# Tiles of one expert each, with a short float32 form for an expert's remainder, in a fused attention and routed-experts kernel

## The chip, the cores and the metric

The kernel runs on one core of a Trainium2 chip. The metric is the device time of one execution in microseconds (us), the median of several runs. A profile is taken of one more execution; times in the rows below count from the start of that execution's span.

## What is computed

The reference is attention inside chunks of 64 positions, followed by a layer of eight experts of which each position uses one. Cut to what matters:

```python
# attention: B=8, H=8, S=576, D=64; chunks of 64 along S
scores = (q_c @ k_c.T) / sqrt(D); attn = softmax(scores); out = attn @ v_c
x = out laid out as (B, S, 512)

# experts: E=8, w1 (8, 512, 1024), w2 (8, 1024, 512)
for b in range(B):
    for s in range(S):
        e = argmax(x[b,s] @ w_gate), or the expert of s-1 if sigmoid(x[b,s] @ w_local) >= 0.5
        h = maximum(x[b,s] @ w1[e], 0)
        out[b,s] = softmax(x[b,s] @ w_gate)[e] * (h @ w2[e])
```

There are 4608 rows (B times S). With the inputs of this case the reference's routing gives the experts 0 to 7 these numbers of rows: 758, 284, 1040, 266, 704, 64, 816, 676.

## The kernel before, in words

The first part computes attention and the router's logits and writes x with the logits to a buffer in DRAM (`x_d`). A drain phase finishes the last attention blocks and, interleaved by a hand-written order (`PAR["drain"]`), sorts the rows by expert: `route` finds each row's expert and its rank in it, `offsets` and `experts` turn the counts into tables on VectorE, and `slots` inverts the assignment with one-hot matmuls into gather and scatter indices. Three early tiles of 128 rows of expert 0 (`EARLY`) run inside that drain.

Then comes the loop over tiles of 128 sorted rows (`step`). Slots are handed out in half tiles of 64 rows (`HT`), an expert gets at least two of them, and the upper half of a tile may belong to another expert than the lower one; such a tile is called mixed. The program has a fixed number of steps; steps from `TMIN` = 36 on are conditional on a register (`valid`), and a table row read into registers (`regs`) tells for each tile whether it is mixed (`mixed`), and whether the next tile's weights differ (`refill`).

A tile's products are made at near float32 accuracy from two-part operands: x, h, w1 and w2 are each kept as a rounded part (hi) and a remainder (lo), and a product is three matmul passes. `mm1` makes h from x and w1 with 24 matmuls of 512 columns, `relu` (ScalarE) takes it out of PSUM, `h_parts` transposes it with eight transposes and makes hi (ScalarE) and lo (VectorE), `mm2` makes y with 24 more matmuls, and `emit_y` scales y by the row's probability on VectorE and scatters it from GpSimd's queue. `x_parts` does the same for x with four transposes. In step t TensorE does, in this order: `mm1` of tile t, the transposes of x of t+1, `mm2` of t-1, the transposes of h of t. In a tail step the transposes of the first half of h stand between the two halves of `mm2`, and x of t+1 is transposed inside the step's first block.

Weights: `raw1` and `raw2` hold the float32 weights of the next expert, one copy. When the next tile has another expert, `refill(0, t)` in step t (after the relu and x of t+1) splits `raw1` into `w1h` and `w1l` (ScalarE makes hi; VectorE makes lo of three pieces, GpSimd of one) and has SyncE load the following expert's w1 into `raw1`, piece by piece behind each split. `refill(1, t)` does it for w2 in step t+1, behind `mm2` and `emit_y` of t.

For a mixed tile the upper 64 rows need the next expert, whose weights are still only in `raw1` and `raw2`. `mm1_upper` and `mm2_upper` make those rows' products in plain float32 from x or h rejoined on GpSimd (`rejoin`), on 64 columns of the array, the two halves of the output columns on the two column halves of the array; this comes on top of the full product of the tile. `relu_mixed` and `y_mixed` put the halves together. All of that stands in conditional blocks (`either`).

Of the kernel before, what the change touches and what calls it, by code (L numbers as in the profile page):

```python
# [21 lines left out]
E, F = 8, 1024  # L22
# [10 lines left out]
NTILE = (2 * EARLY + 1 + 2 * (E - 2) + N // HT + 1) // 2  # L33
# [32 lines left out]
def tile_attention_then_moe(ctx: ExitStack, tc, q, k_in, v, wg, wl, w1, w2, out):  # L66
# [267 lines left out]
    def route(t0, t1, rh_eng):  # L334
# [79 lines left out]
        def rank():  # L414
# [9 lines left out]
                lambda: V.tensor_single_scalar(ri[:, 0], ri[:, 2], HT - 1, ALU.bitwise_and),  # L424
                lambda: V.tensor_single_scalar(ri[:, 1], ri[:, 2], 6, ALU.logical_shift_right),
# [94 lines left out]
    iota_r = iota([P, P], [[1, P]], dst=pa2.tile([P, P], BF16, name="iota_r", tag="xT", bufs=1))  # L520
    iota_m = iota([P, P], [[0, 2], [1, HT]], dt=BF16, name="iota_m")
    iota_h = iota([P, 2, NTILE], [[1, 2], [2, NTILE]], dt=BF16, name="iota_h")
    iota_hp = cpool.tile([P, NTILE], BF16, name="iota_hp")
    for r in range(2):
        nc.gpsimd.iota(iota_hp[HT * r:HT * r + HT], [[2, NTILE]], base=r, channel_multiplier=0,
                       allow_small_or_imprecise_dtypes=True)
    iota_t = iota([P, NT], [[1, NT]], dt=BF16, name="iota_t")
    iota_e = iota([P, E], [[1, E]], name="iota_e")
    idxm8 = iota([P, E], [[1, E]], base=-E, name="idxm8")
    padidx = iota([P, NTILE], [[P, NTILE]], base=2 * N, cm=1, name="padidx")  # L530
    upper = pa1.tile([P, P], BF16, name="upper")
    nc.vector.tensor_scalar(upper, iota_r, pcol, None, ALU.is_gt)
# [13 lines left out]
    def slots(pool, q0, q1, halves, qs, tags=({}, {}, {})):  # L546
# [3 lines left out]
        def s1(n):  # L550
            t0, t1 = halves[n]
            T = t1 - t0
            qv[n] = pool[0].tile([P, T, 2, 2, Q], BF16, name=f"qv{q0}_{n}", **dict(bufs=1) | tags[n])
            qeq = pool[2].tile([P, 2, T, Q], BF16, name=f"qeq{q0}", **dict(bufs=1) | tags[2])
            for r in range(2):
                V.tensor_tensor(qeq[:, r], qs[:, t0:t1].unsqueeze(2).to_broadcast([P, T, Q]),
                                iota_h[:, r, q0:q1].unsqueeze(1).to_broadcast([P, T, Q]), ALU.is_equal)
            for r in range(2):
                V.tensor_scalar(qv[n][:, :, r, 1], qeq[:, r], pcol1, None, ALU.mult)
                V.tensor_tensor(qv[n][:, :, r, 0], qeq[:, r],  # L560
                                iota_t[:, t0:t1].unsqueeze(2).to_broadcast([P, T, Q]), ALU.mult)

        def s2():
            pinv = trp()
            last = halves[-1][1] - 1
            for n, (t0, t1) in enumerate(halves):
                for t in range(t0, t1):
                    nc.tensor.matmul(pinv[:, 0:4 * Q], rh[:, t], qv[n][:, t - t0].rearrange("p r a b -> p (r a b)"),
                                     start=(t == 0), stop=(t == last))
            inv = pool[1].tile([P, 2, Q], F32, name=f"inv{q0}", bufs=1)  # L570
            for r in range(2):
                rows = slice(HT * r, HT * r + HT)
                V.tensor_copy(inv[rows], pinv[rows, 2 * Q * r:2 * Q * r + 2 * Q].rearrange("p (a b) -> p a b", a=2))
            id1 = pool[1].tile([P, Q], F32, name=f"id1{q0}", bufs=1)
            V.scalar_tensor_tensor(id1, inv[:, 0], float(P), inv[:, 1], ALU.mult, ALU.add)
            gi = pa1.tile([P, Q], I32, name=f"gidx{q0}")
# [83 lines left out]
    def mm2_upper(hf, ym):  # L660
        for f in range(8):
            for j in range(2):
                nc.tensor.matmul(ym[HT * j:HT * j + HT, 0:256], hf[f // 4][:, f % 4],
                                 raw2[f // 2][:, f % 2, 256 * j:256 * j + 256], start=(f == 0), stop=(f == 7))
# [7 lines left out]
    def either(mix, plain, both):  # L672
        if mix is None:
            plain()
            return
        with tc.If(mix != 0) as cmp:  # L676
            both()
        with cmp.Else():
            plain()

    def y_mixed(ysb, y, ym, pr):
        V.tensor_scalar(ysb[0:HT], y[0:HT], pr[0:HT], None, ALU.mult)
        for j in range(2):
            V.tensor_copy(ysb[HT:P, 256 * j:256 * j + 256], ym[HT * j:HT * j + HT, 0:256])
        V.tensor_scalar(ysb[HT:P], ysb[HT:P], pr[HT:P], None, ALU.mult)

    def new_m():
        return ps_l.tile([P, 512], F32, name="m", tag="lg")

    def relu_mixed(hsb, hs, hm):  # L690
        nc.scalar.activation(hsb[0:HT], hs[0:HT].rearrange("p j f -> p (j f)"), AF.Relu)
        for j in range(2):
            nc.scalar.activation(hsb[HT:P, 512 * j:512 * j + 512], hm[HT * j:HT * j + HT], AF.Relu)

    def relu(hsb, hs):
        nc.scalar.activation(hsb, hs.rearrange("p j f -> p (j f)"), AF.Relu)  # L696

# [5 lines left out]
    def x_parts(xg, late=False):  # L703
        xp = part("xp", "pT" if late else None)
        hilo(lambda n: xg[:, P * n:P * n + P], xp[:, 0], xp[:, 1])
        return xp[:, 0], xp[:, 1]

    def h_parts(hsb, g, late=False):
        hp = part(f"hp{g}", "xs" if late else None)
        hilo(lambda n: hsb[:, 512 * g + P * n:512 * g + P * n + P], hp[:, 0], hp[:, 1])  # L710
        return hp[:, 0], hp[:, 1]

    def emit_y(t, y, pr, mix=None, ym=None):
# [282 lines left out]
```

## Time and profile before

| what | us |
|---|---|
| median of 3 runs | 722.82 |
| lowest and highest of them | 721.42, 724.65 |
| the profiled execution | 719.68 |
| its span, first to last instruction | 717.9 |
| TensorE (PE) busy in the span | 660.5 |
| VectorE (DVE) busy | 375.4 |
| ScalarE (ACT) busy | 272.3 |
| GpSimd (POOL) busy | 178.7 |

The span lies 1.8 us below the profiled execution's own time, and that execution 3.1 us below the median of the runs. PE and PEld are TensorE's matmuls and weight loads; a float32 matmul leaves two records of each, a matmul of the two-part passes one. A granted clock of 1.00 is 2.4 GHz, 0.50 is 1.2 GHz. Ends of matmuls are modelled, so starts are compared with starts.

### The profile page before, as it was taken

To read this page: it belongs to the slowest core of one execution; us is meant where nothing else is said; L and a number is where in the kernel's file an instruction comes from. 1 tells how busy PE (TensorE), PEld (TensorE's weight loads), DVE (VectorE), ACT (ScalarE), POOL (GpSimd) and SP (SyncE) were. 2 spreads that over 40 slices of the span, in tenths; PEclk is the share of its full clock that TensorE was granted. 3 is DMA by queue.
4 is the path that set the end of the run, shared out by engine and by line. 5 is a ranking of instruction groups with operands and counts; after the bars stand their busy time and mean duration, and the time that the engine had idled before them with its cause. 6 is when DMAs were issued, how large, how long until landed. Compare 5 with 4: busy or idle time off the path is not lost. (4 is left out here: it accounts for less than half of the span.)

```text
span 717.9 us, 17209 instructions
## 1 busy us (share of the span) xinstructions
PE 660.5 (92%) x5630; PEld 525.4 (73%) x5630; DVE 375.4 (52%) x893; ACT 272.3 (38%) x432; POOL 178.7 (25%) x222
## 2 busy tenths in 40 slices
PE   4799898768999999999999999999989999998981
PEld 3688786656777788777888887778878888776860
DVE  2576576686784675455232653562586323455320
ACT  3577575546312244432222444412454222432210
POOL 4332222151031223232111332231243212132110
PEclk9999999889999999999999999999999999999997
DMA  8999999955612244234111451441376210234100
GB/s 219 253 256 258 235 266 266 264 181 155 212 47 103 76 150 147 74 119 163 33 61 32 121 175 58 147 161 45 94 241 225 75 47 31 82 113 163 34 32 17
DMA packets 102671, 97.47 MB, mean 136 GB/s; under 512 B 42416, under 2 KB 79280, under 8 KB 102512
## 3 DMA queue, kind: packets, MB, share of 16 engines
q1 hardware_dynamic: 96352, 75.69, 36.9%
q0 software_dynamic: 6160, 19.85, 8.2%
q8 instruction: 77, 1.26, 0.7%
q14 instruction: 82, 0.67, 0.3%
HBM read 76.48 MB, written 19.56 MB: 134 GB/s over the span
## 5 line engine op out<-in xcount | busy, mean ns | idle before, releaser
L657 PE MATMUL y<-w2h,hp 128*128 128x512 f32 x608 | 203.1, 404 | 9.6 <-DVE hp L607 7.2
L643 PE MATMUL h<-w1h,xp 128*128 128x512 f32 x608 | 178.2, 402 | 0.0
L657 PEld LDWEIGHTS y<-w2h,hp 128*128 128x128 f32 x608 | 114.2, 189 | 38.8 <-DVE hp L607 9.5
L643 PEld LDWEIGHTS h<-w1h,xp 128*128 128x128 f32 x608 | 111.4, 189 | 23.8 <-ACTq L878 0.2
L657 PE MATMUL y<-w2l,hp 128*128 128x512 f32 x304 | 120.5, 396 | 0.0
L716 POOL DMA_INDIRECT out<-ysb,sidx x38 | 41.2, 1085 | 270.1 <-DVEq L878 194.4
L643 PE MATMUL h<-w1l,xp 128*128 128x512 f32 x304 | 95.8, 396 | 0.0
L606 ACT CAST hp<-tr 128x512 fp32r<-128x512 f32 x76 | 41.2, 589 | 108.0 <-PE tr L604 102.6
L607 DVE TENSOR_TENSOR xp<-tr,xp 128x512 fp32r<-128x512 f32 x39 | 27.0, 691 | 103.8 <-ACTq L878 66.6
L715 DVE TENSOR_SCALAR ysb<-y,ppr 128x512 f32<-128x512 f32 x35 | 26.2, 748 | 89.9 <-PE y L657 83.2
L643 PEld LDWEIGHTS h<-w1l,xp 128*128 128x128 f32 x304 | 57.0, 188 | 14.7 <-DVEq L878 0.4
L657 PEld LDWEIGHTS y<-w2l,hp 128*128 128x128 f32 x304 | 57.6, 189 | 12.3
L696 ACT ACTIVATE hsb<-h 128x1024 f32<-128x1024 f32 x35 | 35.9, 1027 | 66.2 <-PE h L643 63.6
L607 DVE TENSOR_TENSOR hp<-tr,hp 128x512 fp32r<-128x512 f32 x76 | 49.3, 686 | 13.4 <-ACT hp L606 12.4
L629 ACT ACTIVATE pex<-pex 128x8 f32<-128x8 f32 x38 | 7.9, 209 | 122.4 <-DVE pex L628 115.7
L97 DVE TENSOR_TENSOR w1l<-raw,w1h 128x1024 fp32r<-128x1024 f32 (+1 forms) x29 | 40.9, 1440 | 13.0 <-ACT w1h L96 13.0
L610 POOL DMA_INDIRECT xg<-x_d,gidx x36 | 36.9, 1025 | 42.8 <-issue 24.7
L246 PE MATMUL o<-v,pT 64*64 64x65 f32 x1152 | 29.7, 235 | 13.3 <-DVE xs L260 7.4
L97 DVE TENSOR_TENSOR w2l<-raw,w2h 128x1024 fp32r<-128x1024 f32 x21 | 40.6, 1988 | 1.2 <-issue 1.2
L604 PE MATMUL tr<-ident,hsb 128*128 128x128 f32 x304 | 40.2, 273 | 0.1
L604 PEld LDWEIGHTS tr<-ident,hsb 128*128 128x128 f32 x304 | 35.3, 140 | 6.5 <-ACT w2h L96 1.2
L159 POOL COPY qr<-qt 128x512 f32<-128x512 f32 x34 | 19.9, 616 | 80.3 <-issue 43.9
(181 smaller groups left out, 838.9 us busy)
## 6 DMA issues: line engine op xcount, KB each, us to landing
raw<-in_moe_w SPq DMA_DIRECT2D x72, 512.0 KB, 4.4
x_d<-xs SPq DMA_DIRECT2D x18, 521.0 KB, 5.4
v<-in_v SPq DMA_DIRECT2D x32, 256.0 KB, 5.3
qt<-in_q SPq DMA_DIRECT2D x11, 512.0 KB, 5.8
kt<-in_k SPq DMA_DIRECT2D x11, 512.0 KB, 7.4
qt<-in_q SPq DMA_DIRECT2D x16, 128.0 KB, 3.1
kt<-in_k SPq DMA_DIRECT2D x16, 128.0 KB, 3.2
qt<-in_q SPq DMA_DIRECT2D x6, 256.0 KB, 4.8
```

The costliest lines, as they stand in the source:

```text
L97: (lo_eng or nc.vector).tensor_tensor(lo, raw, hi.bitcast(F32), ALU.subtract)
L159: eng.tensor_copy(dst, src)
L246: nc.tensor.matmul(o[64 * cp:64 * cp + 64, cc, DV * h:DV * h + D + 1], pT[64 * cc:64 * cc + 64, 4 * j + h, 64 * cp:64 * cp + 64], vt[64 * ...
L604: nc.tensor.transpose(ps[:, n], src_of(n), ident)
L606: return [tr, lambda: nc.scalar.copy(hi, box["ps"]), lambda: V.tensor_tensor(lo, box["ps"], hi.bitcast(F32), ALU.subtract)]
L607: lambda: V.tensor_tensor(lo, box["ps"], hi.bitcast(F32), ALU.subtract)]
L610: nc.gpsimd.indirect_dma_start(out=dst, out_offset=None, in_=src, in_offset=bass.IndirectOffsetOnAxis(ap=gidx[t].bitcast(U32), axis=0))
L643: nc.tensor.matmul(hs[:, j], xs[a][:, c], W1[w][c][:, 512 * j:512 * j + 512], start=(c == 0 and n == 0), stop=(c == 3 and n == 2))
L657: nc.tensor.matmul(y, hx[f // 4][a][:, f % 4], W2[w][c][:, f % 2, :], start=(f == 0 and n == 0), stop=(f == 7 and n == 2))
L696: nc.scalar.activation(hsb, hs.rearrange("p j f -> p (j f)"), AF.Relu)
L715: either(mix, lambda: V.tensor_scalar(ysb, y, pr, None, ALU.mult), lambda: y_mixed(ysb, y, ym, pr))
L716: nc.gpsimd.indirect_dma_start(out=out, out_offset=bass.IndirectOffsetOnAxis(ap=sidx[t].bitcast(U32), axis=0), in_=ysb, in_offset=None, bo ...
```

## The change

Every tile now holds rows of one expert only, at least one tile for each expert. An expert's remainder, the rows that don't fill a tile, comes first among its tiles. A remainder of at most 64 rows makes its tile of kind 1, one of at most 32 rows kind 2. Such a tile is computed in plain float32 from the raw weights alone, with the output columns spread over halves (kind 1) or quarters (kind 2) of the array's columns, and then the expert's weights are split for its full tiles. An expert with a single tile can be of such a kind if the expert after it starts with one too. Expert 0, whose first tiles are the early ones, has no such tile. Mixed tiles, `rejoin` and the additions are gone. Cut to its core:

```diff
-NTILE = (2 * EARLY + 1 + 2 * (E - 2) + N // HT + 1) // 2
+NTILE = EARLY + (N + (E - 1) * (P - 1)) // P
...
-            qv[n] = pool[0].tile([P, T, 2, 2, Q], BF16, ...)
+            qv[n] = pool[0].tile([P, T, 2, Q], BF16, ...)
...
-                    nc.tensor.matmul(pinv[:, 0:4 * Q], rh[:, t], ...)
+                    nc.tensor.matmul(pinv[:, 0:2 * Q], rh[:, t], ...)
...
-    def mm1_upper(xf, hm):
+    def mm1_part(xf, hs, M):
+        n = F * M // P
         for c in range(4):
-            for j in range(2):
-                nc.tensor.matmul(hm[HT * j:HT * j + HT], xf[:, c], raw1[c][:, 512 * j:512 * j + 512],
+            for j in range(P // M):
+                nc.tensor.matmul(hs[M * j:M * j + M, 0, 0:n], xf[:, c, 0:M], raw1[c][:, n * j:n * j + n],
                                  start=(c == 0), stop=(c == 3))
...
-    def mm2_upper(hf, ym):
+    def mm2_part(hf, y, M):
+        n = C * M // P
         for f in range(8):
+            g, b = divmod(f, M // 16)
+            for j in range(P // M):
+                nc.tensor.matmul(y[M * j:M * j + M, 0:n], hf[:, b, M * g:M * g + M],
+                                 raw2[f // 2][:, f % 2, n * j:n * j + n], start=(f == 0), stop=(f == 7))
...
+    def either(kind, plain, partial):
+        if kind is None:
+            plain()
+            return
+        with tc.If(kind != 0) as cmp:
+            with tc.If(kind != 1) as small:
+                partial(P // 4)
+            with small.Else():
+                partial(P // 2)
+        with cmp.Else():
+            plain()
...
+    def y_part(ysb, y, pr, M):
+        n = C * M // P
+        for a in ((HT,) if M == HT else (HT, M)):
+            V.memset(ysb[a:P if a == HT else HT], 0.0)
+        V.tensor_scalar(ysb[0:M, 0:n], y[0:M, 0:n], pr[0:M], None, ALU.mult)
+        for j in range(1, P // M):
+            V.tensor_copy(ysb[0:M, n * j:n * j + n], y[M * j:M * j + M, 0:n])
+        V.tensor_scalar(ysb[0:M, n:C], ysb[0:M, n:C], pr[0:M], None, ALU.mult)
+    def relu_part(hsb, hs, M):
+        nc.scalar.activation(hsb[:, 0:F * M // P], hs[:, 0, 0:F * M // P], AF.Relu)
...
+    def split4(ps, p):
+        nc.scalar.copy(p[:, 0], ps)
+        V.tensor_tensor(p[:, 1], ps, p[:, 0].bitcast(F32), ALU.subtract)
+    def x_parts(xg, kind, late=False, own=False):
         xp = part("xp", "pT" if late else None)
+        ps = trp().rearrange("p (n t) -> p n t", n=4)
+        for n in range(4):
+            nc.tensor.transpose(ps[:, n], xg[:, P * n:P * n + P], ident)
+        xf = pc.tile([P, 4, HT], F32, name="xf", **own_tag("xf", own))
+        plain_only(kind, lambda: split4(ps, xp), lambda: nc.scalar.copy(xf, ps[:, :, 0:HT]))
+        return xp[:, 0], xp[:, 1], xf
+    def h_parts(hsb, g, kind, late=False, own=False):
...
+        def plain():
+            turn(4)
+            split4(ps, hp)
+        def partial(M):
+            turn(M // 16)
+            nc.scalar.copy(hf[:, 0:M // 16], ps[:, 0:M // 16])
+        if g == 0:
+            either(kind, plain, partial)
+        else:
+            plain_only(kind, plain)
...
+    def kinds():
+        c, n, o = cnt[0:1], ntf[0:1], toff[0:1]
+        V.scalar_tensor_tensor(rem, n, -float(P), c, ALU.mult, ALU.add)
+        V.tensor_tensor(first, o, n, ALU.subtract)
+        V.tensor_scalar(some, first, EARLY + 0.5, None, ALU.is_gt)
+        V.scalar_tensor_tensor(some, rem, 0.5 - HT, some, ALU.is_le, ALU.mult)
+        V.memset(lone, 1.0)
+        V.scalar_tensor_tensor(lone[:, 0:E], n, 1.5, some, ALU.is_gt, ALU.mult)
+        V.scalar_tensor_tensor(lone[:, 0:E], n, 1.5, lone[:, 1:E + 1], ALU.is_gt, ALU.max)
+        V.tensor_tensor(some, some, lone[:, 0:E], ALU.mult)
+        V.scalar_tensor_tensor(kind8, rem, 0.5 - 3 * P // 4, some, ALU.is_le, ALU.mult)
+        V.tensor_tensor(kind8, kind8, some, ALU.add)
...
+        lambda: (V.tensor_tensor(wt[:, 0:NTILE], te[0:1], kt[:, 1], ALU.subtract),
+                 V.tensor_copy(wt[:, NTILE:NTILE + 1], wt[:, NTILE - 1:NTILE])),
+        lambda: V.tensor_tensor(regs[:, 0], wt[:, 1:NTILE + 1], wt[:, 0:NTILE], ALU.not_equal),
...
-    def mixed(t):
-        return reg(3, t, 1, [ET.PE, ET.Pool, ET.Activation, ET.DVE]) if t < NTILE else None
+    LAST = TMIN + 5
+    def kind_of(t):
+        return reg(3, t, 2, [ET.PE, ET.Activation, ET.DVE])
...
-                plain = lambda: [mm1(xps[t], hs, c) for c in range(4)]
-                either(mix[t], plain, lambda: (plain(), mm1_upper(full[0, t], hm)))
+                either(kind[t], lambda: [mm1(xps[t], hs, c) for c in range(4)],
+                       lambda M: mm1_part(xps[t][2], hs, M))
...
             if cs[-1] == 3:
-                emit_y(t - 1, y, prc[t - 1], mix[t - 1], ym)
+                either(kind[t - 1], plain, lambda M: mm2_part(hps[t - 1][0][2], y, M))
+                emit_y(t - 1, y, prc[t - 1], kind[t - 1])
+            else:
+                plain_only(kind[t - 1], plain)
```

`turn(k)` makes k transposes of h. `wt` is the expert whose split weights are in place during a tile: for a partial tile the one before its own. `plain_only` is `either` with one arm for both kinds, or none. The register with the kind is read by PE, ACT and DVE before `mm1` of the tile before; POOL no longer reads it.

## Rows read from the trace of the kernel before

**Rows 1.** From the page: busy time, share of the span and instructions of each engine, and the granted clock of TensorE in 40 slices of the span, in tenths.

```profile
PE 660.5 (92%) x5630; PEld 525.4 (73%) x5630; DVE 375.4 (52%) x893; ACT 272.3 (38%) x432; POOL 178.7 (25%) x222
...
PEclk9999999889999999999999999999999999999997
```

**Rows 2.** Busy time by stage, one stretch of full and mixed tiles: the stretch and its length, then busy us of PE, PEld, DVE, ACT and POOL (instructions), TensorE's granted clock, DMA's share and GB/s.

```profile
254.00:384.00 130.00, 128.58 (x654) 102.22 (x653) 62.04 (x129) 42.82 (x65) 32.01 (x26) 1.00 0.33 103
```

**Rows 3.** Groups of instructions by line and form: line, engine, operation, out<-in, shape, count, then busy us and mean ns of one, and idle time before.

```profile
L657 PE MATMUL y<-w2h,hp 128*128 128x512 f32 x608 | 203.1, 404 | 9.6 <-DVE hp L607 7.2 <-ACTq L899 1.2 <-PEq L899 0.8
...
L651 PE MATMUL m<-raw,fullx 128*64 128x512 f32 x48 | 11.0, 598 | 0.0
```

**Rows 4.** PE's timeline from a full tile to a mixed one: start, length in us, engine, line, operation, out<-in, shape, count.

```profile
273.44 0.72 PE L643 MATMUL h<-w1h,xp 128*128 128x512 f32 x2
...
279.15 0.60 PE L604 MATMUL tr<-ident,xg 128*128 128x128 f32 x4
...
285.19 1.04 PE L604 MATMUL tr<-ident,hsb 128*128 128x128 f32 x8
285.98 0.72 PE L643 MATMUL h<-w1h,xp 128*128 128x512 f32 x2
...
291.77 3.65 PE L651 MATMUL m<-raw,fullx 128*64 128x512 f32 x16
295.36 0.66 PE L604 MATMUL tr<-ident,xg 128*128 128x128 f32 x4
...
314.07 3.67 PE L663 MATMUL m<-raw,full 128*64 128x256 f32 x32
317.68 1.09 PE L604 MATMUL tr<-ident,hsb 128*128 128x128 f32 x8
```

**Rows 5.** PE's timeline in the attention part, where it works on parts of the array: the router's logits (L289, a quarter of the columns each) and the scores (L197, quarters of 64 by 64), each with the row that follows.

```profile
133.82 0.64 PE L289 MATMUL lg<-xT,wg 128*32 128x256 f32 x8
134.39 0.23 PE L391 MATMUL tr<-ident,eT 18*128 18x18 f32 x1
...
137.79 1.16 PE L197 MATMUL sc<-kT,qT 64*64 64x64 f32 x64
138.88 1.09 PE L167 MATMUL tr<-ident,xs 128*128 128x128 f32 x8
```

**Rows 6.** PE's timeline in the tile loop, the rows with an idle time over 1.3 us before them (in brackets, with the releaser).

```profile
326.72 0.72 PE L657 MATMUL y<-w2h,hp 128*128 128x512 f32 x2 [1.42 <-DVE hp L607]
...
473.69 0.73 PE L657 MATMUL y<-w2h,hp 128*128 128x512 f32 x2 [1.43 <-DVE hp L607]
538.40 0.73 PE L657 MATMUL y<-w2h,hp 128*128 128x512 f32 x2 [1.81 <-DVE hp L607]
...
650.43 0.72 PE L657 MATMUL y<-w2h,hp 128*128 128x512 f32 x2 [2.50 <-DVE hp L607]
```

**Rows 7.** DVE's timeline after the second product of a mixed tile: the first operation on y, the low parts of w2, the low parts of the next h.

```profile
317.79 0.74 DVE L682 TENSOR_SCALAR ysb<-y,ppr 64x512 f32<-64x512 f32 x1 [6.77 <-PE m L663]
...
320.23 5.71 DVE L97 TENSOR_TENSOR w2l<-raw,w2h 128x1024 fp32r<-128x1024 f32 x3 [0.29 <-issue]
325.97 1.29 DVE L607 TENSOR_TENSOR hp<-tr,hp 128x512 fp32r<-128x512 f32 x2
```

**Rows 8.** A split and reload of w1, from the timelines of ACT, DVE and SP (the queue that issues the loads) and from a table of stretches of 1 us (columns as in rows 2; the last two are DMA's share and GB/s).

```profile
295.53 1.02 ACT L691 ACTIVATE hsb<-h 64x1024 f32<-64x1024 f32 x1 [7.14 <-PE m L651]
...
298.27 3.90 ACT L96 CAST w1h<-raw 128x1024 fp32r<-128x1024 f32 x4
...
299.36 1.23 DVE L97 TENSOR_TENSOR w1l<-raw,w1h 128x1024 fp32r<-128x1024 f32 x1 [0.26 <-ACT w1h L96]
301.25 3.81 DVE L97 TENSOR_TENSOR w1l<-raw,w1h 128x1024 fp32r<-128x1024 f32 x2 [0.67 <-ACT w1h L96]
...
300.72 4.81 SPq L883 DMA_DIRECT2D raw<-in_moe_w  x4
...
311.00:312.00 1.00, 1.00 (x6) 0.82 (x5) 0.03 (x1) 0.00 (x0) 0.00 (x0) 1.00 0.58 221
312.00:313.00 1.00, 1.00 (x6) 0.82 (x5) 0.00 (x0) 0.00 (x0) 0.00 (x0) 1.00 0.03 8
```

**Rows 9.** The timeline of SP around expert 5's one tile: two reloads of w1, then two of w2.

```profile
514.60 17.34 SPq L883 DMA_DIRECT2D raw<-in_moe_w  x8
533.70 19.07 SPq L886 DMA_DIRECT2D raw<-in_moe_w  x8
```

**Rows 10.** The table of stretches (columns as in rows 2; the third figure from the right is the granted clock), after the waits of 1.81 and of 2.50 us.

```profile
540.00:543.30 3.30, 3.30 (x10) 2.54 (x8) 1.13 (x4) 2.32 (x4) 0.00 (x0) 0.50 0.99 338
...
651.00:652.00 1.00, 1.00 (x6) 0.82 (x5) 0.62 (x5) 0.61 (x2) 0.00 (x0) 1.00 1.03 399
```

**Rows 11.** The one-hot products of `slots`, by form (columns as in rows 3).

```profile
L568 PE MATMUL tr<-qv,rh 128*128 128x152 bf16 x36 | 2.5, 229 | 0.0
...
L568 PE MATMUL tr<-qv,rh 128*128 128x20 bf16 x36 | 1.3, 172 | 0.0
```

**Rows 12.** The branches of `either` on PE's queue: engine, operation, count, shortest, median and longest ns, first and last start.

```profile
L676 PEldq COMPARE_BRANCH  x157: 68/207/431, 221.0 to 699.5; - x157
```

**Rows 13.** Two operations of the table building on DVE, a large and a small one (columns as in rows 3).

```profile
L834 DVE TENSOR_REDUCE tb<-tb 1x46 f32<-1x368 f32 x1 | 0.5, 524 | 0.0
...
L835 DVE TENSOR_SCALAR regs<-te 1x46 int32<-1x46 f32 x1 | 0.2, 166 | 0.0
```

More of the change, by code (lines that the diff above doesn't have):

```diff
@@ L519, in tile_attention_then_moe @@
     pcol1 = iota([P, 1], [[0, 1]], base=1, cm=1, name="pcol1")
[L520 to L526, printed above, removed]
+    iota_m = iota([P, P], [[1, P]], dt=BF16, name="iota_m")
+    iota_q = iota([P, NTILE], [[1, NTILE]], dt=BF16, name="iota_q")
     iota_t = iota([P, NT], [[1, NT]], dt=BF16, name="iota_t")
     iota_e = iota([P, E], [[1, E]], name="iota_e")
+    later = cpool.tile([P, E], F32, name="later")
+    nc.gpsimd.memset(later, 1.0)
+    nc.gpsimd.memset(later[:, 0:1], 0.0)
     idxm8 = iota([P, E], [[1, E]], base=-E, name="idxm8")
@@ L718, in emit_y @@
             in_=ysb, in_offset=None, bounds_check=N - 1, oob_is_err=False)
-    xgs, xps, hps, prc, full, hsbs = {}, {}, {}, {}, {}, {}
+    xgs, xps, hps, prc, hsbs = {}, {}, {}, {}, {}
     def early_gather():
@@ new lines, in tile_attention_then_moe @@
+    rem, first, some, kind8 = (bt([1, E], n) for n in ("rem", "first", "some", "kind8"))
+    lone = bt([1, E + 1], "lone")
+    ehot = pc.tile([P, NTILE, E], F32, name="ehot", bufs=1)
+    def kinds():
[10 more added lines that the diff above has]
+        V.tensor_tensor(kind8, kind8, some, ALU.add)
@@ L948, in step, with next_x @@
                     next_h(g)
-            full[1, t] = [rejoin(mix[t], *hps[t][g], g) for g in range(2)]
-    def next_x(t, mix):
-        mix[t] = mixs[t] if t in mixs else mixed(t)
+    def next_x(t):
         if EARLY < t <= TMIN:
-            xps[t] = x_parts(xgs[t], t == TMIN)
-        full[0, t] = rejoin(mix[t], *xps[t], "x")
+            xps[t] = x_parts(xgs[t], kind[t], t == TMIN)
         refill(0, t - 1)
@@ L961, in tile_attention_then_moe @@
     with tc.manual_schedule(engines=MAN | {ET.SP, ET.Pool}):
-        mix, ok = {}, {EARLY: None, EARLY + 1: None}
-        oks, mixs = {}, {}
-        next_x(EARLY, mix)
-        for t in range(EARLY, TMIN + 3):
-            step(t, ok, mix)
+        kind, ok = {EARLY: None}, {EARLY: None, EARLY + 1: None}
+        next_x(EARLY)
+        for t in range(EARLY, LAST + 1):
+            step(t)
             n = t - EARLY
             if 20 <= t < 26:
-                oks[t + 16] = valid(t + 16)
-                mixs[t + 16] = mixed(t + 16)
+                ok[t + 16] = valid(t + 16)
+                kind[t + 16] = kind_of(t + 16)
             run(sl[n:n + 1])
-        with when(ok[TMIN + 2]):
-            for t in range(TMIN + 3, NTILE + 1):
-                step(t, ok, mix)
+        with when(ok[LAST]):
+            for t in range(LAST + 1, NTILE + 1):
+                step(t)
 _INS = ["q", "k", "v", "moe_w_gate", "moe_w_local", "moe_w1", "moe_w2"]
```

140 lines of the change are left out of this document (60 added, 80 removed).

## The prediction

> **What bounds the kernel now.** I read the page first, then the stages, then PE's own timeline and its waits. PE is busy for 660.5 us of a span of 717.9 us, at a granted clock near its upper level of 2.4 GHz [rows 1]. The stage table shows where the rest is not: in the stretch of expert tiles from 254 to 384 us PE is busy for 128.58 of 130 us, and DVE, ACT and POOL each for less than half of it [rows 2]. So a full tile costs what its matmuls cost. PE's timeline gives that price: from one tile's first L643 matmul at 273.44 to the next one's at 285.98 is 12.54 us, of which the first product takes 5.7 us, four transposes of x 0.35, the second product 5.7 and eight transposes of h 0.8 [rows 4]. There are 38 such tiles (608 first-weight matmuls, 16 in a tile) and three of them are mixed (48 records of L651, 16 in a tile) [rows 3]. A mixed tile adds 3.59 us (291.77 to 295.36) and 3.61 us (314.07 to 317.68) [rows 4]. Only four waits of PE over 1.3 us stand in the tile loop: 1.42, 1.43, 1.81 and 2.50 us, 7.2 us in all, each for DVE's low part of h behind a split of w2 [rows 6].
>
> **How many tiles after.** From the rows per expert (758, 284, 1040, 266, 704, 64, 816, 676): tiles of one expert each are 6, 3, 9, 3, 6, 1, 7, 6 = 41. Remainders are 118, 28, 16, 10, 64, 64, 48, 36 rows. Expert 0's remainder is not treated; experts 1, 2 and 3 get a quarter tile (32 rows), experts 4, 5, 6 and 7 a half tile (64 rows). Of the 41 tiles 34 are full, three of them early ones as before. So the loop goes from 35 full tiles, three with additions, to 31 full and 7 partial ones.
>
> **The work on PE.** Removed: 4 x 12.54 = 50.2 us, and 3 x 7.2 = 21.6 us of additions. A half tile issues the very matmuls of the mixed additions, alone: 0.35 + 3.59 + 0.4 (four transposes of h) + 3.61 = 7.95 us, four times 31.8. For a quarter tile the trace has no such product, but the router's L289 has its form: eight records of 128*32 by 256 columns take 0.57 us from start to start (133.82 to 134.39) [rows 5]. Four such sets make the first product: 2.3 us at most, and 1.8 us if sets follow without a gap, as half tiles show (half of 3.59). I take 1.8. The second product has 64 records of 128 columns; that PE issues small records fast enough is seen in L197, 64 records in 1.09 us [rows 5]. Between 1.8 and 3.6 (no better than a half tile) I take 1.8, the nearer to these rows. So 0.35 + 1.8 + 0.2 + 1.8 = 4.15 us, three times 12.5 (up to 19.5). Net: -50.2 - 21.6 + 31.8 + 12.5 = **-27.5 us** (-20.5 at the other end). Switches between full and partial array, 14 of them at 0.08 us (the gap seen before 291.77): +1.1, from 0 to 4.
>
> **The slots.** Each of 36 products of the last slot stage has 74 columns in place of 152. The row of 152 columns takes 2.5 us, that of 20 columns 1.3 [rows 11]; I take -1.1 us, between 0 and -1.2.
>
> **Waits that go.** With the mixed tiles go their waits, and with another order at experts 5 and 6 the fourth one: -7.2 us. After the 1.81 us wait the clock fell to half for 540.00 to 543.30 [rows 10], which cost half of 3.3 us: -1.7. The 2.50 us wait was followed by no fall. Together -8.9.
>
> **Waits that come, at a usual boundary.** After the second product of a partial tile, DVE evacuates y, splits w2 and only then makes the next tile's low part of h. In a mixed tile y took from 317.79 to 319.9, the split 5.71 us, and the first low part was there at 326.66 [rows 7], 8.9 us after that product ended; PE wants it 7.55 us after (0.8 transposes, 5.7 first product, 0.35, two matmuls). For a half tile y is shorter (three operations on half the columns, about 1.2 us against 2.1), which leaves a wait of 0.5 us: expert 4, +0.5. For a quarter tile the product ends 1.8 us earlier, but DVE must first take the next x and clear two row blocks (until about 0.9 us after that end), and y has five small operations (1.4 us). With the split and the low part, 0.3 + 5.7 + 0.7, that is 9.0 us against the same 7.55: about 1.6 us of wait, three times, +4.8 (0 to 7.5). One in four waits of this size cost half-speed time: +1.3. Expert 7's partial tile is followed by a tail step, where the transposes of h stand before the second product and wait for a relu of 1.02 us [rows 8]: +0.9. The w1 split at a partial tile is covered: PE has 0.35 + 5.7 + 0.3 us of work, the first low part is done 2.3 us after the split's start and the last 6.8 us after it [rows 8], and the product takes a quarter of them every 1.4 us.
>
> **Waits that come at experts 5 and 6.** This is the large term. Expert 5 is one partial tile, and expert 6's partial tile comes straight behind. Both read the raw weights, so expert 6's raw w1 must land between two neighbouring tiles. Today the two reloads of w1 are a full tile apart (eight issues in 17.34 us) and no wait for a load is seen [rows 6, 9]. From a split's start at 298.27 the four loads are issued from 300.72 to 305.5, each behind its own split, and DMA goes quiet just before 312: 13.6 us [rows 8]. Call T0 the end of expert 5's first product. The split starts 1.1 us later (relu, copy of x), so the load is complete at T0 + 14.7 and expert 6's last quarter of the product ends at about T0 + 15.6. Without the wait it would end at 0.35 + 5.7 + 0.4 + 3.6 = T0 + 10.05. Wait: 5.5 us. Then the same for w2, and worse, since DVE does expert 6's w1 split first. Call T1 the end of that product. The split starts at T1 + 1.5, so DVE is free at T1 + 8.3, has y done at 9.6, and splits w2 until 15.5 (scatter and POOL's share between); the last load is issued then and lands 5.3 to 6.7 us later, about T1 + 21.3; the product ends at 22.2 in place of 14. Wait: 8.3 us (6 to 9). While PE waits that long the clock will fall as it did after 1.81 us: the two last quarters at half speed cost 0.9 us each, and the half-speed stretch after the second wait 1.7 us. Sum +17.3 us, between 8 and 20.
>
> **Drain.** DVE prepares the tile tables there. The lists get some 14 more operations of about 0.17 us and one more of 0.52 [rows 13], 2.9 us, and the slots of that stage lose one comparison and two products of the same size class, 1.3 us. PE follows DVE there with little room; I take +1.0, from 0 to 2.5. POOL loses its additions and its branches; it was idle enough that this changes nothing.
>
> **Sum.** -27.5 + 1.1 - 1.1 - 8.9 + (0.5 + 4.8 + 1.3 + 0.9) + 17.3 + 1.0 = -10.6 us. The profiled execution took 719.7 us, so its like would take 709; the median of the runs is 3.1 us above the profiled one, so I forecast **712 us**.
>
> **Rivals.** (a) The raw weights of expert 6 come in time, because loads that compete with nothing land sooner or because the split is reordered by its waits. Then some 17 us of the added waits are absent: 695 us. Against it stands the chain in [rows 8], in which every load is behind its own split. Chance 0.12.
>
> (b) The boundary waits are larger: each of six w2 splits costs PE 2 us more and half-speed time follows most. +11: 723 us, no change. For it speaks that DVE and POOL lengthen each other's splits (three low parts take 5.71 us, two 3.81 [rows 7, 8]). Chance 0.22.
>
> (c) The other side: every full tile pays for branching past larger arms. Each step keeps seven conditional blocks, and the code that a full tile jumps over grows in the second product from 56 matmul records (24 of the full product and 32 of the addition) to 96 (64 of the quarter arm, 32 of the half arm). Today a branch takes PE's queue 207 ns, at most 431 [rows 12], and nothing of it shows as idle time of PE [rows 2]. If each of 31 full tiles paid 0.43 us the gain of 10.6 and the 3.6 us that a measurement can tell would be used up; from there it is slower, and at 1 us a tile it is 743 us. Chance 0.11. The Trainium skill has a rule that speaks for this one: "Runtime: NRT & Kernel Launch", section on instruction fetch mechanics, says that a taken branch whose target lies outside the fetched window waits for a DMA fetch. By that rule this rival could hold; the trace so far shows jumps of this kind without a gap, which is why its chance stays low.
>
> (d) The array's quarters do not run side by side in the products. As halves at best: 3 x 3.6 = +11, 723 us; one after another +32, 744 us. L289 speaks against it. Chance 0.05.
>
> **Chances and range.** My forecast has 0.50, with its own range 705 to 719. A difference under 0.5% (3.6 us) is about what a measurement of this kernel can't tell from none. Faster: 0.50 + 0.12 + the lower edge of (b) = 0.66. Same: most of (b) and part of (d), 0.20. Slower: (c) and the rest, 0.14. The range leaves out most of (a) and of (c): 701 to 725.
>
> **What would show it.** Right: 31 + 3 full tiles in the records of L643 and L657's successors, half products of about 3.6 us and quarter products of about 1.8; full tiles still 12.5 us apart; two waits of PE for a DMA of raw weights, of about 5 and 8 us, near expert 5, with the clock at half after them; small waits for DVE's low part behind each quarter tile. Wrong: no wait for raw weights (a), waits of 3 us and more at each expert (b), full tiles of 13 us and more with PE waiting for its own queue (c), or quarter products as long as half ones (d).

## The result, and the profile after

The change is slower by 0.8%: 727.08 us median (721.33 to 731.37, 20 runs) against 721.49 (714.45 to 724.65, 20 runs) for the kernel before, ratio 1.0078, 95% interval 1.0049 to 1.0106. The forecast was 712 us (701 to 725) and faster. The profiled execution took 731.37 us, span 729.6; of its 11.7 us over the span before, 4.1 are already there at a transpose of the attention stage where both kernels run the same code (L356 starts at 198.43 us against 194.34). From the start of the last slot product to the end it is 465.8 us (729.6 - 263.79) against 459.3 (717.9 - 258.59). I call this stretch the tail stretch below; it is what a profile tells best, and the whole time is told by the runs.

TensorE's row of the page and its granted clock, as in [rows 1]: 16 us less work than before, and yet a longer span.

```profile
PE 644.2 (88%) x5776; PEld 507.1 (69%) x5776; DVE 375.3 (51%) x925; ACT 268.0 (37%) x434; POOL 178.2 (24%) x218
...
PEclk9999999988999999999999999999999899999997
```

A full tile on PE's timeline (columns as in [rows 4]), from one first product to the next: 12.35 us against 12.54. Full tiles do not pay for longer jumps; their first product is even 0.16 us shorter (why, no run here shows).

```profile
340.59 0.71 PE L635 MATMUL h<-w1h,xp 128*128 128x512 f32 x2
...
346.14 0.60 PE L719 MATMUL tr<-ident,xg 128*128 128x128 f32 x4
...
352.15 1.04 PE L731 MATMUL tr<-ident,hsb 128*128 128x128 f32 x8
352.94 0.48 PE L635 MATMUL h<-w1h,xp 128*128 128x512 f32 x1
```

Partial products: a quarter tile's first product takes 1.86 us (265.49 to 267.35), its second 1.95 to the last record's end; a half tile's 3.58 (449.42 to 453.00) and 3.61 (470.14 to 473.75).

```profile
265.49 1.93 PE L643 MATMUL h<-raw,xf 128*32 128x256 f32 x32 [0.28 <-issue]
267.35 0.66 PE L719 MATMUL tr<-ident,xg 128*128 128x128 f32 x4
...
449.42 3.65 PE L643 MATMUL h<-raw,xf 128*64 128x512 f32 x16
453.00 0.66 PE L719 MATMUL tr<-ident,xg 128*128 128x128 f32 x4
...
470.14 3.67 PE L657 MATMUL y<-raw,hf 128*64 128x256 f32 x32
473.75 0.44 PE L731 MATMUL tr<-ident,hsb 128*128 128x128 f32 x2
```

Product by product the work came out as forecast. What did not is the idle time. PE's timeline, rows with an idle time over 0.5 us before them (as [rows 6], where four rows stood):

```profile
275.31 0.70 PE L635 MATMUL h<-w1h,xp 128*128 128x512 f32 x2 [1.50 <-ACTq L682]
282.38 1.95 PE L657 MATMUL y<-raw,hf 128*32 128x128 f32 x64 [0.94 <-SPq L926]
286.62 0.70 PE L635 MATMUL h<-w1h,xp 128*128 128x512 f32 x2 [0.85 <-ACT w2h L96]
...
305.32 0.47 PE L649 MATMUL y<-w2h,hp 128*128 128x512 f32 x1 [2.29 <-DVE xp L713]
314.60 0.70 PE L635 MATMUL h<-w1h,xp 128*128 128x512 f32 x2 [1.69 <-issue]
333.04 0.73 PE L649 MATMUL y<-w2h,hp 128*128 128x512 f32 x2 [1.96 <-DVE hp L713]
424.71 0.70 PE L635 MATMUL h<-w1h,xp 128*128 128x512 f32 x2 [1.50 <-ACTq L682]
...
462.46 0.70 PE L635 MATMUL h<-w1h,xp 128*128 128x512 f32 x2 [2.79 <-issue]
...
537.58 4.66 PE L643 MATMUL h<-raw,xf 128*64 128x512 f32 x12 [2.01 <-issue]
...
551.11 0.70 PE L635 MATMUL h<-w1h,xp 128*128 128x512 f32 x2 [1.72 <-ACT w2h L96]
562.89 1.98 PE L657 MATMUL y<-raw,hf 128*64 128x256 f32 x8 [5.64 <-DMA raw<-in_moe_w]
...
645.16 0.71 PE L635 MATMUL h<-w1h,xp 128*128 128x512 f32 x2 [0.94 <-ACTq L682]
```

Seven of them, 275.31, 314.60, 424.71, 462.46, 537.58, 551.11 and 645.16, stand before the first product that follows a partial tile: 12.1 us, of which the forecast had none. What PE's queue does in the first of them, by line, over 272 to 276 us (engine, operation, count, ns, first and last start):

```profile
L682 PEldq EVENT_SEMAPHORE  x1: 51/51/51, 273.8 to 273.8; - x1
L682 PEldq COMPARE_BRANCH  x1: 179/179/179, 274.0 to 274.0; - x1
...
L921 PEldq TENSOR_LOAD <-regs x1: 303/303/303, 274.2 to 274.2; - x1
L921 PEldq FUSED_REGOPS  x1: 146/146/146, 274.6 to 274.6; - x1
...
L670 PEldq COMPARE_BRANCH  x1: 222/222/222, 274.9 to 274.9; - x1
```

L682 is the branch around the second half of h, whose arm is empty for a partial tile. The queue waits there on a semaphore that PE itself raises: it comes at 273.8, when the transposes of the first half, which stand in the arm before, end (273.42 + 0.38). Then the branch, the read of the next tile's kind (L921) and the next branch (L670) follow, one behind the other, with an idle array. At tile 21 two reads more (the loop reads six kinds and flags early there) make it 2.79 us.

### The profile page after: what moved, and what is told of

Its sections match the earlier page's. It is cut to its first block, busy times and chain, and to the rows that moved or that the text cites. A ratio compares the mean times of both kernels' runs of the same rounds, so it can differ in the third digit from the quotient of the medians.

```text
span 729.6 us, 17751 instructions
## 1 busy us (share of the span) xinstructions
PE 644.2 (88%) x5776; PEld 507.1 (69%) x5776; DVE 375.3 (51%) x925; ACT 268.0 (37%) x434; POOL 178.2 (24%) x218
## 3 DMA queue, kind: packets, MB, share of 16 engines
q8 instruction: 99, 1.62, 0.9%
## 5 line engine op out<-in xcount | busy, mean ns | idle before, releaser
L649 PE MATMUL y<-w2h,hp 128*128 128x512 f32 x544 | 183.5, 407 | 9.5 <-DVE hp L713 3.1
L635 PE MATMUL h<-w1h,xp 128*128 128x512 f32 x544 | 157.9, 400 | 13.5 <-issue 4.5
L649 PEld LDWEIGHTS y<-w2h,hp 128*128 128x128 f32 x544 | 103.4, 191 | 36.0 <-DVE hp L713 5.2
L635 PEld LDWEIGHTS h<-w1h,xp 128*128 128x128 f32 x544 | 100.0, 190 | 35.3 <-ACT w2h L96 6.1
L649 PE MATMUL y<-w2l,hp 128*128 128x512 f32 x272 | 108.4, 398 | 0.0
L635 PE MATMUL h<-w1l,xp 128*128 128x512 f32 x272 | 84.8, 393 | 0.0
L712 ACT CAST hp<-tr 128x512 fp32r<-128x512 f32 x62 | 33.7, 587 | 112.7 <-PE tr L731 112.7
L635 PEld LDWEIGHTS h<-w1l,xp 128*128 128x128 f32 x272 | 51.3, 189 | 11.4
L713 DVE TENSOR_TENSOR hp<-tr,hp 128x512 fp32r<-128x512 f32 x62 | 40.4, 687 | 18.9 <-ACT hp L712 15.6
L602 POOL DMA_INDIRECT xg<-x_d,gidx x39 | 43.6, 1119 | 17.7 <-issue 9.6
L246 PE MATMUL o<-v,pT 64*64 64x65 f32 x1152 | 29.5, 235 | 11.7 <-DVE xs L260 8.3
```

What stands on the lines that cost most here:

```text
L246: nc.tensor.matmul(o[64 * cp:64 * cp + 64, cc, DV * h:DV * h + D + 1], pT[64 * cc:64 * cc + 64, 4 * j + h, 64 * cp:64 * cp + 64], vt[64 * ...
L602: nc.gpsimd.indirect_dma_start(out=dst, out_offset=None, in_=src, in_offset=bass.IndirectOffsetOnAxis(ap=gidx[t].bitcast(U32), axis=0))
L635: nc.tensor.matmul(hs[:, j], xs[a][:, c], W1[w][c][:, 512 * j:512 * j + 512], start=(c == 0 and n == 0), stop=(c == 3 and n == 2))
L649: nc.tensor.matmul(y, hx[f // 4][a][:, f % 4], W2[w][c][:, f % 2, :], start=(f == 0 and n == 0), stop=(f == 7 and n == 2))
L712: nc.scalar.copy(p[:, 0], ps)
L713: V.tensor_tensor(p[:, 1], ps, p[:, 0].bitcast(F32), ALU.subtract)
```

## Experiments

All ratios are to the kernel before, timed beside each version on the same chip; the change itself is 1.0078.

**The transposes ahead of the branch.**

```diff
-        def turn(k):
-            for n in range(k):
-                nc.tensor.transpose(ps[:, n], ...)
+        for n in range(4):
+            nc.tensor.transpose(ps[:, n], ...)
         def plain():
-            turn(4)
             split4(ps, hp)
         def partial(M):
-            turn(M // 16)
             nc.scalar.copy(hf[:, 0:M // 16], ps[:, 0:M // 16])
```

> One edit to the changed kernel (727.1 us median): the four transposes of h in h_parts stand ahead of the branch for both halves of h, as those of x do in x_parts, and the arms hold only the copies, so that leaving an arm waits for no result of TensorE. A partial tile then makes eight transposes where it made two or four: at 0.11 us each 3 x 0.66 + 4 x 0.44 = 3.7 us more. Theory A (the idle stretches before the first product that follows a partial tile, 1.50, 1.69, 1.50, 2.79, 2.01, 1.71 and 0.94 us, are a drained TensorE queue: the end of the empty arm waits for TensorE's own transposes, and the branch, the register read and the next branch that were hidden stand behind it): these stretches fall below 0.5 us each, 727.1 - 12.1 + 3.7 = 718.7 us, between 715 and 723. Theory B (the split of w1 by ScalarE and VectorE is late there): the stretches stay, and the extra transposes fall into them or add to them, 727 to 731 us.

716.17 us, ratio 0.9978 (0.9955 to 1.0001): 1.0% below the change, some 7 us where theory A has 8.4 (12.1 less 3.7 of added transposes). The idle time of 1.50 us behind tile 6 is gone from PE's timeline; its first rows over 0.5 us are now

```profile
276.35 1.95 PE L657 MATMUL y<-raw,hf 128*32 128x128 f32 x64 [1.80 <-SPq L923]
281.25 0.70 PE L635 MATMUL h<-w1h,xp 128*128 128x512 f32 x2 [1.69 <-ACT w2h L96]
...
550.38 6.13 PE L657 MATMUL y<-raw,hf 128*64 128x256 f32 x32 [7.43 <-DMA raw<-in_moe_w]
```

Part of the gain went into other waits: 0.94 became 1.80, and at expert 6, 5.64 became 7.43: from the end of expert 5's first product to the end of expert 6's second it is 40.4 us (516.02 to 556.44) against 41.1 (528.90 to 570.00), though the change has two of its seven waits there, 2.01 and 1.72 us. The loads set the time of this stretch.

**The kind read behind the first product.**

```diff
-        if t + 1 < NTILE and t + 1 not in kind:
+        if t >= TMIN and t + 1 < NTILE and t + 1 not in kind:
             kind[t + 1] = kind_of(t + 1)
...
                        lambda M: mm1_part(xps[t][2], hs, M))
+                if t + 1 < NTILE and t + 1 not in kind:
+                    kind[t + 1] = kind_of(t + 1)
```

> One edit to the changed kernel: the register that says the kind of tile t + 1 is read behind the first product of tile t, as the kernel before read it, and not ahead of it (the last tiles, whose registers are read early, stay as they are). Theory A (drained queue): the read and what is worked out from it took 0.7 us of each stretch before the product that follows a partial tile (274.2 to 275.0 us in the trace for tile 6), so seven stretches shrink by 0.4 to 0.7 us each, 727.1 - 4 = 723 us, between 721 and 725. Theory B (w1 split late): no change, 727 us.

721.82 us, ratio 1.0064 (1.0041 to 1.0087). In place it did what theory A said: 1.50 us behind tile 6 became 0.82, and the seven together 7.9 us in place of 12.1. In the whole it is 0.14% less, inside what the runs can tell.

**w1 without its low part.**

```diff
-                split(hi[c], lo[c], raw[c], nc.gpsimd if c == 1 else nc.vector)
+                if which == 0:
+                    nc.scalar.copy(hi[c], raw[c])
+                else:
+                    split(hi[c], lo[c], raw[c], nc.gpsimd if c == 1 else nc.vector)
```

> The changed kernel without the low part of w1 at a refill: only ScalarE's copy runs there, VectorE's and GpSimd's subtractions (1.2 us and 2.5 us each) are left out, so the products use a stale low part; the loads of the next raw weights start earlier. Theory B (w1 split late holds the product behind a partial tile): the stretches of 0.94 to 2.79 us before it go, 727 - 12 = 715 us, ratio 0.991. Theory A (drained queue of TensorE): they stay; only what hangs on the landing of the loads gains, 2 to 3 us: 724 to 727 us, ratio 1.003 to 1.008.

714.34 us, ratio 0.9963 (0.9939 to 0.9986): between the two theories' numbers and outside both, so the total alone would mislead. PE's timeline decides:

```profile
269.98 0.70 PE L635 MATMUL h<-w1h,xp 128*128 128x512 f32 x2 [1.51 <-ACTq L682]
...
307.95 0.70 PE L635 MATMUL h<-w1h,xp 128*128 128x512 f32 x2 [1.62 <-issue]
...
416.32 0.70 PE L635 MATMUL h<-w1h,xp 128*128 128x512 f32 x2 [1.50 <-ACTq L682]
...
453.81 0.70 PE L635 MATMUL h<-w1h,xp 128*128 128x512 f32 x2 [2.80 <-issue]
```

Four waits of 1.50, 1.69, 1.50 and 2.79 us stayed at 1.51, 1.62, 1.50 and 2.80 without any subtraction: theory B falls. The gain, more than theory A had for it, stands where loads start earlier: before expert 6's second product 5.64 us of wait became 1.44 and 0.82, and the waits of 0.94 us before second products are gone.

**No partial form for an expert of one tile.**

```diff
-        V.scalar_tensor_tensor(lone[:, 0:E], n, 1.5, some, ALU.is_gt, ALU.mult)
-        V.scalar_tensor_tensor(lone[:, 0:E], n, 1.5, lone[:, 1:E + 1], ALU.is_gt, ALU.max)
+        V.tensor_scalar(lone[:, 0:E], n, 1.5, None, ALU.is_gt)
```

> One edit to the changed kernel: an expert of one tile never runs it in the partial form (the second line of the lone rule is gone), so expert 5's only tile is a full one with split weights, and expert 6's partial tile 28 no longer follows another partial tile. If the two partial tiles in a row cost what the trace shows (w1 late by 2.0 and 2.7 us, w2 by 5.64 and 3.5 us, 0.97 us more: 14.8 us) because the raw weights can only be loaded from one partial tile to the next, then 727.1 - 14.8 + (12.4 - 8.0) for the full tile = 716.7 us, between 713 and 720. Rival: the loads of expert 6 are late behind any single-tile expert, and the wait moves to tile 28 as it is: 727 to 732 us.

716.65 us, ratio 0.9971 (0.9948 to 0.9995): 1.07% below the change, 7.7 us of the 10.4 expected. PE has no wait for a load of raw weights any more.

**No partial tile at all.**

```diff
+        V.memset(kind8, 0.0)
```

> One edit to the changed kernel: no tile is of the partial kind (the kinds are set to zero), 41 full tiles of one expert each, the same code with its branches. TensorE's work grows by 3 x (12.4 - 4.4) + 4 x (12.4 - 8.0) = 41.6 us. If the partial tiles bring waits of their own of about 40 us (12 before the next first product, 15 at the lone expert, 4 at tile 9, 7 around the second products, the stretches at half clock behind them) and ordinary boundaries cost 1 to 2 us each: 727.1 + 41.6 - 40 + 8 = 737 us, between 728 and 745. Rival (most of those waits belong to any change of expert, not to the partial form): 750 to 768 us.

719.55 us, ratio 1.0027 (1.0010 to 1.0045): 0.5% *faster* than the change, against 737 expected. So seven partial tiles, with 41.6 us less work by the timeline, are worth less than nothing as the change runs them. The whole stretch of tiles in one row each (columns as in [rows 2]), first with full tiles only, then the change:

```profile
260.00:719.00 459.00, 442.72 (x2167) 363.87 (x2165) 210.99 (x440) 149.08 (x229) 113.58 (x84) 0.99 0.32 105
```

```profile
264.00:729.00 465.00, 416.83 (x2269) 324.16 (x2265) 212.16 (x450) 144.08 (x226) 111.29 (x85) 0.97 0.31 104
```

PE is busy for 25.9 us less in the change, part of it at the lower clock (0.97 against 0.99), and idle for 48.2 us in place of 16.3. Up to 690 us the full-tile version has a single wait of PE over 0.5 us, 1.94 us at 543.13. A change of expert costs PE next to nothing; my 8 us for usual boundaries in this expectation were wrong. The waits belong to the partial form.

**Halves in place of quarters.**

```diff
-        V.tensor_tensor(kind8, kind8, some, ALU.add)
+        V.tensor_copy(kind8, some)
```

> One edit to the changed kernel: every partial tile runs on halves of the columns, none on quarters. Work alone: 3 x (3.59 - 1.86 + 3.60 - 1.95) = 10.1 us more, 737 us, ratio to before 1.022. If the quarter tiles leave TensorE's queue no time to run ahead (a first product of 1.86 us, behind which the exit's branch, 2.87 us at tile 9, stands bare, and products at half clock behind it), 2 to 3 us of each come back: 727 + 10.1 - 8 = 729 us, ratio 1.008 to 1.014.

724.26 us, ratio 1.0093 (1.0059 to 1.0128), no different from the change: 10 us more work for nothing lost. The quarter tiles bring their savings back as waits: over 258.7 to 723 us PE is idle for 40.3 us here, against 48.2 in the change's row above.

**Three edits together.** Those of the first, the second and the fourth experiment in one version.

> The three edits together: the transposes of h ahead of the branch, the kind read behind the first product, no partial form for an expert of one tile. Alone they measured 0.9978, 1.0064 and 0.9971 of the kernel before, against 1.0078 for the change, so 1.0 %, 0.14 % and 1.07 % less. If they take away different waits they add, less the wait before the product behind tile 27 that both the first and the third remove (2.0 us): 1.0078 - 0.0100 - 0.0014 - 0.0107 + 0.0028 = 0.9885 of before, between 0.984 and 0.992. Rival: the branch that leaves a short arm and the landing of the loads hold the same places, so that what one edit frees the next wait takes: 0.993 to 0.998.

708.19 us, ratio 0.9874 (0.9842 to 0.9906). They add, and this version beats both kernels. It also lies 1.5% below the version with full tiles only, so the partial form does pay once most of its waits are gone. The tail stretch is some 448 us.

**The arms in the other order.** On top of the three edits.

```diff
-        with tc.If(kind != 0) as cmp:
+        with tc.If(kind == 0) as cmp:
+            plain()
+        with cmp.Else():
             with tc.If(kind != 1) as small:
                 partial(P // 4)
             with small.Else():
                 partial(P // 2)
-        with cmp.Else():
-            plain()
```

> e4_all with the arms of the choice in the other order: the full tile's arm first in the code, the partial arms behind it, so that leaving a partial arm no longer jumps over the full tile's 96 products. If the long branches of TensorE (2.87 us at tile 9, 1.18, 1.56 and 1.69 us elsewhere, all at the end of a partial arm; 0.2 us is the usual one) come from that jump, they shrink to 0.2 us, and the places where they stood bare (2.3 us at tile 9, 0.9 us and 1.7 us before first products) gain: 2 to 5 us less than e4_all. Rival: the jump is only moved to the arm's entry, or full tiles now pay at their exit 34 times: the same as e4_all or up to 10 us more.

710.90 us, ratio 0.9900 (0.9870 to 0.9930), not told apart from the three edits without it: the rival held, and the long branch moved. In the change it took 2.87 us from 302.3 (L670): not at a partial arm's end, as the expectation has it, but at the choice ahead of tile 8's full second product, right behind tile 9's quarter product. Here the longest is 4.80 us, at the choice between the partial arms (L673). The two rows, of the change over 300 to 306 us and of this version, with the shortest, median and longest ns:

```profile
L670 PEldq COMPARE_BRANCH  x2: 73/1472/2872, 301.3 to 302.3; - x2
```

```profile
L673 PEldq COMPARE_BRANCH  x45: 70/176/4796, 258.9 to 637.8; - x45
```

**w1's loads behind w2's refill.** On top of the three edits, with the arms in the first order. The four loads leave the refill of w1 and stand in a branch of their own at the step's end.

```diff
             refill(1, t - 1)
+            if t + 1 < NTILE:
+                load_raw1(t)
```

> e4_all with one more edit: the loads of the next raw w1 are issued behind the refill of w2 of the same step, in a branch of their own, and not inside the refill of w1; what the refills split and load stays the same. Theory C (the wait before a partial second product is SyncE's: it leaves the w2 refill's arm, in which it has nothing to do, only when the w1 loads it issued just before have landed, and the partial product waits for SyncE to have come past it): the idle stretches before the partial second products of e4_all, 1.32, 0.85, 1.14, 2.09 and 0.74 us, fall below 0.3 us: 5 us less than e4_all, ratio to before 0.9874 - 0.007 = 0.980, between 0.977 and 0.984. Rival (these products wait for data, ScalarE's copy of h or the raw w2): the stretches stay, 0.985 to 0.990.

726.28 us, ratio 1.0086 (1.0050 to 1.0123): 2% slower than the three edits, outside what either theory forecast. Theory C held in its place, but the wait moved. The waits of 0.86 to 2.09 us before second products in the loop are gone; new ones stand before partial first products, and the last is ended by SyncE leaving the new branch:

```profile
446.74 3.53 PE L643 MATMUL h<-raw,xf 128*64 128x512 f32 x8 [2.75 <-SPq L921]
...
545.26 5.05 PE L643 MATMUL h<-raw,xf 128*64 128x512 f32 x14 [12.73 <-SPq L921]
```

```profile
L921 SPq EVENT_SEMAPHORE  x4: 17/17/17, 542.0 to 545.1; - x4
...
  PE h L643: 12.7, 1
```

SyncE stands in the branch's empty arm on four semaphores until 545.1, behind the loads of w2 that it issued from 533.77 to 538.6. In the change it is the same with the roles exchanged: it issues w1's loads up to 277.2, stands in the empty arm of w2's refill until 282.3, and the partial second product starts at 282.38. SyncE's loads and its semaphores over 280.7 to 282.35 us there:

```profile
272.45 4.77 SPq L931 DMA_DIRECT2D raw<-in_moe_w  x4
```

```profile
L926 SPq EVENT_SEMAPHORE  x4: 17/17/17, 280.7 to 282.3; - x4
...
  PE y L657: 0.9, 1
```

**Halves only, with these loads, and with the loads as they were.** The quarter arms are left out of the code.

> e10_loads without the form on quarters, its arms left out of the code: all partial tiles run on halves. Work: 10.1 us more than e10_loads; transposes the same. If the quarters' work counts in full once the drained queue and the loads are out of the way: ratio 0.980 + 0.014 = 0.994. If, as with every partial tile on halves in the changed kernel (1.0093 against 1.0078), the short products only make room for waits (a long branch at their exit, products at half clock behind them): 0.980 to 0.986.

722.59 us, ratio 1.0037 (1.0012 to 1.0062), 0.5% below the quarters' version; the two intervals overlap.

> e4_all without the form on quarters, its arms left out of the code: all partial tiles run on halves, the loads as in e4_all. Work: 10.1 us more than e4_all (0.9874). If the quarters' work counts in full: 1.001. If, as e11 against e10 showed (0.5 % less), the quarters' short first product brings back what its work saves (long branches behind it, products at half clock): 0.982 to 0.988.

713.18 us (711.59 without one run of 719.14), ratio 0.9889 (0.9838 to 0.9940), the same as 0.9874 within its interval. Three pairs of quarters against halves, and in none do the quarters show their 10 us (1.4%).

**w1's loads one step later.** `load_raw1(t - 1)` behind the first product of step t.

> e12_half with the loads of the next raw w1 issued one step later, behind the first product of that step and ahead of the refill of w2, in a branch of their own. Theory C (a partial product waits for SyncE to leave an empty arm, and that for the landing of the loads issued before it): neither the partial second products (by the order of the refill of w2 and these loads) nor, other than in e10_loads, the partial first products (for the landing of w2) wait for SyncE; what is left is the raw w1 itself, late where an expert has one tile: the waits before the partial second products of e12_half go, 4 to 5 us, and tile 28's first product may wait for its data up to 5 us: 0.977 to 0.985, not above e12_half by more than 0.3 %. Rival (the loads must start early, whatever waits for them): as in e10_loads, 1 to 2 % above e12_half.

711.50 us, ratio 0.9882 (0.9843 to 0.9921). In place as theory C says: no wait of PE for SyncE over 0.5 us is left, and the stretch is 448.0 us (707.6 - 259.60) against 450.3 (714.0 - 263.73). In the whole the runs can't tell the two apart, and the 0.977 to 0.985 of theory C was not reached.

## Why the prediction was wrong

**Right.** The count of tiles, 34 full and 7 partial ones. The work: half tiles as forecast, quarter tiles about 4.4 us against 4.15, side by side on the array, so rival (d) falls. Rival (c) falls as it was put: full tiles are 12.35 us. The low part of h behind w2's split: 0.49, 1.96 and 0.69 us, a stretch at half clock of 1.8 us and 0.99 us for the relu in the tail step, 5.9 us in all against 7.5 forecast (whose 1.6 us for a quarter tile should be 1.45 by its own figures, 9.0 less 7.55). Experts 5 and 6: 2.7 us for w1 and 9.2 for w2 (5.64 of wait and 3.5 of a slower product), 11.9 against 17.3. Three more waits stand in the same stretch and are counted below, 2.01, 1.72 and 0.61 us; with them it is 16.2, and the 41.1 us of the stretch compare with 39.6 by the forecast (15.6, 22.2 and twice 0.9). So this term held, in mechanism and nearly in size.

**The step that failed** is "the w1 split at a partial tile is covered". It looked for data only. The split was covered (the subtractions left out change nothing there), but what PE waits for before the next first product is its own queue: 12.1 us, priced at nothing. (Some 3.7 of them stand at experts 5 and 6, where by the first experiment the loads hold PE anyway.) Every conditional block was priced by [rows 12], 207 ns of queue time that ran behind 5.7 us of products. A partial tile has no such products behind it, and its empty arm ends with a wait for PE's own results, after which nothing runs ahead. Putting the transposes ahead of the branch took back 7 us.

**What else was missing.** Before partial second products 0.94 and 0.94 us, for SyncE and its landing loads, and 0.61 us, where the profile names ScalarE's relu. Before the first products after those 0.85, 0.38, 1.51 and 0.59, the first of them a branch of 0.75 us; what the others wait for, no run here separates. At tile 9 a branch of 2.87 us, from 302.3, behind a first product of 1.86 us that is too short to cover it: 2.29 us of idle time. The profile names DVE's low part of x, done at 305.20, but the branch too ends at 305.2, and tile 8's second product does not read that x. In the second, third and fourth experiment this product again starts 0.16 or 0.17 us after the branch (1.57, 2.40 and 2.36 us there), and in the first, where no branch at this place is over 0.33 us, it doesn't wait. Products at half clock behind such waits:

```profile
305.00:312.60 7.60, 7.28 (x25) 5.78 (x26) 5.22 (x4) 3.65 (x4) 2.46 (x1) 0.78 0.48 156
...
332.00:340.00 8.00, 6.96 (x24) 5.53 (x25) 3.35 (x11) 1.71 (x3) 0.00 (x0) 0.79 0.60 216
462.00:470.00 8.00, 7.54 (x28) 6.06 (x28) 1.20 (x7) 0.33 (x2) 1.97 (x2) 0.79 0.53 193
```

The clock column is a mean over stretches at the upper level and at half of it; the first products at 462.46 took 7.15 us in place of 5.55 and the second at 305.32 7.21 in place of 5.66. For the tail stretch of the profiled executions this gives 12.1 + 2.5 + 3.3 + 2.3 + 3.2 = 23.4 us unforeseen, less 5.4 at experts 5 and 6, 1.6 at the low part of h and some 4 on full tiles, plus 0.8 of quarter tiles: 13 of the 18 us between the forecast for it and 465.8 - 459.3. Some 5 us stay without a place.

Rival (b) had the nearer time, 723 us, for another reason (longer w2 splits); rival (c) had the right kind of cause, PE's own queue, at the wrong tiles. I asked of the branches what they cost where products cover them, and not where the change takes the cover away. 
The long branches stay partly open. These are PE's choices at L670 (shortest, median and longest ns) with full tiles only, with halves in place of quarters, and in the version of halves only whose loads are as they were:

```profile
L670 PEldq COMPARE_BRANCH  x184: 169/207/1497, 235.4 to 687.6; - x184
```

```profile
L670 PEldq COMPARE_BRANCH  x183: 68/207/2225, 233.4 to 687.9; - x183
```

```profile
L670 PEldq COMPARE_BRANCH  x218: 68/205/438, 238.1 to 689.0; - x109
```

In the first two no quarter tile runs, and still a branch takes 1.50 and 2.23 us; in the third, whose code has no quarter arms, none is over 0.44 us, and in the two other versions without them none over 0.37. So the long branches go with the quarter arms in the code, run or not. No two versions differ in that alone, and the usual branch takes 0.2 us in all of them. With full tiles only the long ones are covered by products and cost PE no wait over 0.5 us.

The Trainium skill, "Runtime: NRT & Kernel Launch", section on instruction fetch mechanics, says that a jump out of the fetched window waits for a fetch. That the longest branch was another one when the arms had changed places agrees with it, and so do these rows, but no run here shows the fetch as the cause.

## What to carry to other kernels

Before work is moved to a shorter form behind a branch, list what the engine's queue does around it, branches, register reads and semaphores of empty arms, and ask whether enough work is queued to cover it: these tiles saved 41.6 us of work and lost all of it. Keep an engine's own instructions out of arms where they can stand ahead of the branch, and look at what an empty arm waits for, on DMA-issuing engines too. Price a saved instruction by a version without it, as the version with full tiles only did: it would have shown before anything else that the partial form, as it was written, gained nothing.

## What the hardware showed

- Leaving an arm in which an engine had nothing to do cost it a wait for work issued earlier: PE waited for its own transposes (1.5 us with what stands behind), SyncE for the landing of four loads (about 5 us in the change, and 12.7 us of PE's time where the order was turned).
- A register read with its arithmetic is about 0.7 us of PE's queue (303 and 146 ns with the gaps between), a branch on PE usually 0.2 us and here up to 4.8.
- The branches over 0.44 us at PE's choices stood only in versions whose code has the quarter arms, also where no quarter tile ran (up to 2.23 us).
- The gain of one edit is partly taken by the next wait: 12.1 us of idle time removed gave 7 us. The transposes added for it are 3.7 us by the expectation's estimate, and around experts 5 and 6, where the loads set the time, the edit gave 0.7 us in place of 3.7.
